# Half of one store and the loads of one block move behind a tile's first visit, a value load and a second store behind its second visit (retention, then a cosine-gated MLP)

## The chip, the cores and the metric

The kernel runs on one core of one Trainium2 chip. The metric is the device time of that core in microseconds. TensorE (PE in the profile) multiplies matrices, VectorE (DVE) and GpSimd (POOL) do element-wise work, ScalarE (ACT) does activations and copies, and SyncE (SP) only issues DMAs here.

## What is computed

The reference, cut to its core (q, k, v are 8 batches x 8 heads x 576 positions x 64, in float32; `w_in` is 512x2048 and `w_out` 2048x512):

```python
scores = q @ k.transpose(0, 1, 3, 2) / sqrt(64)
ret = scores * Dmat                      # Dmat[h, i, j] = gamma_h ** (i - j) for i >= j, else 0
x = (ret @ v).transpose(0, 2, 1, 3).reshape(4608, 512)
h = x @ w_in
out = (h * cos(h)) @ w_out               # 4608 x 512, float32
```

## The kernel before, in words

**Blocks and tiles.** The 4608 tokens are cut into 18 blocks of 256 (`j`) for the retention and into nine tiles of 512 (`n`, 0 to 8 in the code; the text calls them by this index) for the MLP. Tile n computes its MLP from the retention outputs of blocks 2n and 2n+1, and while it does so the retention of two later blocks, 2n+2 and 2n+3, is finished.

**The retention of a block.** `load` (L133) brings q, k and v of a block into SBUF, from a pool `ld` that holds three blocks. `prep` (L217) scales q and k by powers of gamma on GpSimd (four instructions at L203), and `round_v` (L210) casts v to bfloat16 there (two instructions at L214). `turned` (L225) transposes the scaled q and k on TensorE. `scores` (L287), `sums_of` (L351) and `outputs` (L492, made of `out_own` L433 and `out_carried` L471) are short matmuls with 64-row operands; the matmul at L477 is the last kind of an output.

**The MLP of a tile.** `mm1` (L511) makes h, 64 matmuls of 512 columns per tile (L525); cosine (L538) and product (L539) follow on ScalarE and VectorE. The second product is done by `mm2_seven` (L658) with seven products of quarter matrices in place of eight, in the order x = 1, 2, 6, 4, 7, 5, 3, each of 16 matmuls of 256 columns (L640). Their sums give four output tiles: c11, c21, c22 and u1 (tile buffers `ot`, two for each of the four). ScalarE copies a product out (L670), VectorE adds another to it (L666), and `stored_rows` (L650) writes the tile out by two DMAs of 64 partitions each.

**Where the visits lie.** In tiles 3 to 7 the transposes stand ahead of product 2. The retention's short matmuls stand in two packets, which the code calls a unit and this text a visit: the first (`first_unit`, L1051) ahead of product 4, and the second (`second_unit`, L1054) ahead of product 3, or of 5 in tile 7. A visit issues an output's own part, the state sums and scores of another block, and the output's carried part.

**What sets the order.** Each engine runs its instructions in the order in which the program records them; that order is written by hand. Adds and stores that wait for a product are put in a list `pend` and recorded by `flush`. After c11's store (s = 0) `stored` calls `steps_to` (L767), which records `prep`, `round_v` and the next block's load; the store of u1 (s = 3) does this a second time. All loads and nearly all stores are issued from SP's one queue, so a store that waits for its sum holds back whatever is recorded behind it. Around the first visit the order on SP is thus: both halves of c11's store, loads of q, k and v, then both halves of the stores of c21, of c22 and of u1, then the loads of the other block. Loads exist up to tile 5; then all 18 blocks are in.

Of the kernel before, what the change touches and what calls it, by code (L numbers as in the profile page):

```python
# [17 lines left out]
def kernel(  # L18
# [9 lines left out]
    nc = tc.nc  # L28
# [4 lines left out]
    HP = P // 2  # L33
# [9 lines left out]
    N2 = DM // 2  # L43

    W = 512
    NT = NTOK // W
    last = NT - 1
    BK = 256
    NB = NTOK // BK
# [44 lines left out]
    tiles = {}  # L94
# [23 lines left out]
    def parts_of(t0, n, per):  # L118

        cut = -t0 % S  # L120
        if 0 < cut < n:
            return [(0, cut // per, t0), (cut // per, n // per, t0 + cut)]
        return [(0, n // per, t0)]

    def after(i, gate):
        tc.add_manual_dep(
            i.ins,
            gate.ins.name,
            mybir.DependencyInfo(mybir.DependencyClass.Sync, mybir.DependencyReason.DATA),
            reason="in this order",  # L130
        )

    def load(j, names="qkv", gate=None):  # L133
        for name in names:
            src = {"q": q, "k": k, "v": v}[name]
            if name == "q" or j < NP_B:
                f = ld.tile([P, H, 2, D], F32, tag="f" + name, name=f"f{name}")
                for p0, p1, t in parts_of(j * BK, BK, 2):
                    b, s0 = divmod(t, S)
                    i = nc.sync.dma_start(  # L140
                        f[p0:p1].rearrange("p h r d -> p h (r d)"),
                        src[b, :, s0 : s0 + 2 * (p1 - p0), :].rearrange(
                            "h (p r) d -> p h (r d)", r=2
                        ),
                    )
                    if gate is not None:
                        after(i, gate)
                        gate = None
            else:
                f = ld.tile([P, 2, H, D], F32, tag="f" + name, name=f"f{name}")  # L150
                for y in range(2):
                    for p0, p1, t in parts_of(j * BK + y * P, P, 1):
                        b, s0 = divmod(t, S)
                        i = nc.sync.dma_start(
                            f[p0:p1, y],
                            src[b, :, s0 : s0 + p1 - p0, :].rearrange("h s d -> s h d"),
                        )
                        if gate is not None:
                            after(i, gate)
                            gate = None  # L160
            tiles["f" + name, j] = f
        return i
# [109 lines left out]
    def head(he, hg):  # L272
        return he * HG + hg

    def q_cols(c, he, hg, n):
        return tiles["qkT", c.j][he * D : he * D + D, 0, :, hg, c.p0 : c.p0 + n]
# [194 lines left out]
    def out_carried(j, ps):  # L471
        cs = [c for c in chunks[j] if c.carry]
        for hg in range(0, HG, 2):
            for c in cs:
                for h in [head(he, hg + u) for u in range(2) for he in range(2)]:
                    he = h // HG
                    nc.tensor.matmul(  # L477
                        ov_cols(c, ps, h, c.carry),
                        lhsT=s_before[c][he * D : he * D + D, h % HG, :],
                        rhs=q_cols(c, he, h % HG, c.carry),  # L480
                        start=False,
                        stop=hg > 0 and c is cs[-1],
                        skip_group_check=True,
                    )
# [119 lines left out]
    def late_sums(n, xs):  # L604
        for x in xs:
            g_sum(n, x, 6 if x == 5 and n > 1 else 0 if x == 3 and n == 2 else 4, E2)
# [40 lines left out]
            )  # L647
        return parts

    def stored_rows(r0, c0, c1, t, queues=(nc.sync, nc.sync)):  # L650

        rows = out[r0 : r0 + P * t.shape[1], c0:c1].rearrange(
            "(j i r) c -> r i j c", r=2, i=HP
        )
        for r in range(2):
            queues[r].dma_start(rows[r], t[r * HP : (r + 1) * HP])

    def mm2_seven(n, at, stored, xs=(1, 2, 6, 4, 7, 5, 3), early=None):  # L658
        pend = []

        def flush():
            while pend:
                pend.pop(0)()

        def add(out_, in0, in1):
            return lambda: nc.vector.tensor_tensor(out=out_, in0=in0, in1=in1, op=ALU.add)  # L666

        def copied(tag, x):
            t = op.tile([P, 2, N2], F32, tag=tag, name="ot")
            held.append(lambda ps=tiles["all", x]: nc.scalar.copy(t, ps))  # L670
            return t

        def store(t, r, c, s):
            def go():
                queues = (nc.sync, nc.scalar) if n == last and s else (nc.sync, nc.sync)
                stored_rows(n * W + r * 256, c * N2, (c + 1) * N2, t, queues)
                stored(s)

            return go

        def copies():
            while held:
                held.pop(0)()

        for x in xs:
            if x not in at:
                copies()
                flush()
            else:
                if at[x].__name__ in ("nothing", "first_scores", "last_outputs", "turning"):  # L690
                    copies()
                at[x](flush, pend)
                copies()
            if x == 6 and n > 1:
                late_sums(n, (3,))
            parts = product(n, x, early)
            if x == 1:
                c11 = copied("a", 1)
                tiles["c11"] = c11
                if n > 1:  # L700
                    late_sums(n, (5, 6))
            elif x == 2:
                c11 = tiles["c11"]
                if n == 1:
                    p2 = copied("d", 2)
                    continue
                pend[:0] = [add(c11, c11, tiles["all", 2]), store(c11, 0, 0, 0)]
            elif x == 6:
                u1 = copied("b", 1)
            elif x == 4:  # L710
                c21 = copied("c", 4)
            elif x == 7 and n == 1:
                pend += [
                    add(c21, c21, tiles["all", 1]),
                    add(c22, c22, tiles["all", 1]),
                    store(c21, 1, 0, 1),
                    store(c22, 1, 1, 2),
                    add(c11, c11, p2),
                    store(c11, 0, 0, 0),
                ]  # L720
            elif x == 7:
                c22 = copied("d", 1)
                pend += [add(c21, c21, tiles["all", 1]), store(c21, 1, 0, 1)]
            elif x == 5 and n == 1:
                c22 = copied("d", 5)
            elif x == 5 and n == last:
                for (j, c0, c1), ps in zip(parts, tiles["o", 5]):
                    pend.append(add(c22[:, j, c0:c1], ps, c22[:, j, c0:c1]))
                pend.append(store(c22, 1, 1, 2))
            elif x == 5:  # L730
                pend += [
                    add(c22, c22, tiles["all", 5]),
                    add(u1, u1, tiles["all", 5]),
                    store(c22, 1, 1, 2),
                ]
            elif n < last:
                pend += [add(u1, u1, tiles["all", 5 if n == 1 else 3]), store(u1, 0, 1, 3)]
                flush()
            else:
                flush()  # L740
                copies()
                for (j, c0, c1), ps in zip(parts, tiles["o", 5]):
                    add(u1[:, j, c0:c1], ps, u1[:, j, c0:c1])()
                    if c1 == N2:
                        stored_rows(
                            n * W + j * P, N2, DM, u1[:, j : j + 1, :], (nc.sync, nc.scalar)
                        )

    loaded, prepared = 2, 0
# [7 lines left out]
    def step(then_load=True):  # L757

        nonlocal prepared
        if prepared < NB:  # L760
            prep(prepared)
            round_v(prepared)
            prepared += 1
            if then_load:
                load_next()

    def steps_to(j):  # L767
        while prepared < min(NB, j):
            step()

    def load_w_in(e0, part=None):
        dgs = slice(0, DG) if part is None else slice(2 * part, 2 * part + 2)
# [182 lines left out]
    for n in range(NT):  # L955
# [37 lines left out]
        if n == 0:  # L993
# [28 lines left out]
            for done, (t, e) in enumerate(order):  # L1022
# [9 lines left out]
                for u in range(2 * (t == 1) if t < 2 else 1) if e == ET - 1 else ():  # L1032
                    u = u if t < 2 else t
# [78 lines left out]
        else:  # L1112
            at = {2: turning, 4: first_unit, 3 if b + 1 < NB else 5: second_unit} if n < last else {}

        def stored(u):
            if n == 1:
                if u == 0:
                    step(False)
            else:
                steps_to({0: 2 * n + 6, 3: 2 * n + 7}.get(u, 0))  # L1120

        mm2_seven(n, at, stored, *([(2, 4, 6, 5, 7, 3)] if n == 1 else []))

# [29 lines left out]
```

## Time and profile before

| | |
|---|---|
| median of 3 runs | 293.02 us (292.79 to 293.71) |
| the profiled execution's own time | 292.63 us |
| its span, from first to last instruction | 290.9 us |
| TensorE busy | 284.3 us, 98% of the span |
| VectorE, ScalarE, GpSimd busy | 218.5, 170.7, 147.9 us |
| granted TensorE clock | 1.000 |
| DMA traffic | 42.62 MB, mean 146 GB/s |

Shares are of the span. A busy TensorE is not necessarily at its peak, since matmuls overlap; how fast a stage goes is seen from the chain of waits, which lists pieces of work in order of time with their lengths. The profile names a wait by the engine and line that waited and by what ended the wait. Lines with SPq are DMA issues on SP's queue; their length is the time of issuing and not of the transfer.

### The profile page before, as it was taken

The numbers are of one execution on the slowest core, as the hardware profiler recorded it, in microseconds if no ns is written. First come the engines' busy times: TensorE is split into PE (matmuls) and PEld (weight loads), VectorE is DVE, ScalarE is ACT, GpSimd is POOL, SyncE is SP. The second block draws the span as 40 slices with busy tenths as digits, with TensorE's granted clock in tenths as the row PEclk, the third lists the DMA queues.
The fourth block names the chain that finished last, engine by engine and source line by source line (L and its number), as shares of the span: only waits on it lengthen the run. The fifth ranks groups of instructions, "written<-read, shape, count | busy, mean of one in ns | idle before, by whom it ended". The sixth has DMA issues, their size and how long they took to land.

```text
span 290.9 us, 10529 instructions
## 1 busy us (share of the span) xinstructions
PE 284.3 (98%) x4336; PEld 191.3 (66%) x4336; DVE 218.5 (75%) x309; ACT 170.7 (59%) x200; POOL 147.9 (51%) x169
## 2 busy tenths in 40 slices
PE   7999999999999999999999999999999999999994
PEld 2664446888854786478647874687458845884584
DVE  5767758999967967896789677977698669745943
ACT  6756216756677655676467746673767476536620
POOL 7840435698977993379136923593348024002400
PEclk9999999999999999999999999999999999999999
DMA  7999999997997989837690589139101220122013
GB/s 218 275 171 205 252 235 247 224 220 195 223 224 183 268 207 230 210 78 176 170 227 15 129 200 217 42 99 231 38 0 41 65 49 0 41 51 59 0 38 108
DMA packets 103853, 42.62 MB, mean 146 GB/s; under 512 B 68480, under 2 KB 103296, under 8 KB 103808
## 3 DMA queue, kind: packets, MB, share of 16 engines
q1 hardware_dynamic: 99104, 37.37, 52.5%
q0 software_dynamic: 4256, 4.19, 9.1%
q8 instruction: 36, 0.59, 0.8%
q10 hardware_dynamic: 448, 0.39, 0.4%
q14 instruction: 9, 0.07, 0.1%
HBM read 36.70 MB, written 9.44 MB: 159 GB/s over the span
## 4 chain that ended last, share of the span: by engine, by line
PE 94%; DVE 3%; DMA 1%; issue 0%; ACT 0%; DVEq 0%; ACTq 0%
PE h L525 43%; PE o L640 34%; PE o L1025 5%; PE ov L449 3%; PE tr L239 3%; PE ov L477 2%; PE sc L332 2%; DVE ret L312 1%; PE st L365 1%; DMA fk<-in_k_dram 1%; DVE qks L171 1%; PE sc L299 0%; PE tr L260 0%; ACT ot L670 0%; PE idle L270 0%
## 5 line engine op out<-in xcount | busy, mean ns | idle before, releaser
L525 PE MATMUL h<-xT,w_in_sb 128*128 128x512 bf16 (+1 forms) x656 | 127.4, 353 | 0.0
L539 DVE TENSOR_TENSOR gT<-h,cosh 128x1024 bf16<-128x1024 f32 x72 | 87.8, 1221 | 27.3 <-ACT cosh L538 26.8
L538 ACT ACTIVATE cosh<-h,half_pi 128x1024 f32<-128x1024 f32 x72 | 80.2, 1115 | 40.7 <-PE h L525 40.7
L525 PEld LDWEIGHTS <-w_in_sb 128*128 128x128 bf16 x656 | 63.5, 98 | 58.6 <-DMA w_in_sb<-in_moe_w_in_dram 0.2
L579 POOL TENSOR_TENSOR gs<-gT 128x512 bf16<-128x512 bf16 x30 | 38.1, 1271 | 99.6 <-DVE gT L539 99.0
L640 PEld LDWEIGHTS <-gs 128*128 128x128 bf16 x528 | 49.6, 98 | 5.9
L203 POOL TENSOR_TENSOR qks<-fk,gkc 128x512 bf16<-128x512 f32 x32 | 39.0, 1237 | 5.1 <-DMA fk<-in_k_dram 5.1
L640 PEld LDWEIGHTS <-gT 128*128 128x128 bf16 x384 | 36.6, 98 | 6.1
L666 DVE TENSOR_TENSOR ot<-ot,o 128x512 f32<-128x512 f32 x35 | 23.3, 683 | 20.2 <-ACT ot L670 12.6
L245 ACT COPY qkT<-tr 128x1024 bf16<-128x1024 bf16 x29 | 27.7, 1021 | 12.0 <-PE tr L239 11.0
L203 POOL TENSOR_TENSOR qks<-fq,gq 128x512 bf16<-128x512 f32 x28 | 31.2, 1134 | 4.6 <-DMA fq<-in_q_dram 4.6
L640 PE MATMUL o<-w_out_sb,gs 128*128 128x256 bf16 (+1 forms) x264 | 30.7, 270 | 0.0
L640 PE MATMUL o<-w_out_sb,gT 128*128 128x256 bf16 x256 | 30.6, 273 | 0.0
L640 PE MATMUL o<-ws,gs 128*128 128x256 bf16 (+1 forms) x264 | 30.4, 269 | 0.0
L670 ACT COPY ot<-o 128x512 f32<-128x512 f32 x33 | 19.2, 586 | 18.1 <-PE o L640 17.5
L341 DVE TENSOR_TENSOR ret<-sc,mask_c 128x512 bf16<-128x512 f32 x32 | 20.6, 683 | 7.5 <-PE sc L332 6.6
L214 POOL CAST vb<-fv 128x512 bf16<-128x512 f32 x35 | 22.0, 650 | 6.7 <-DMA fv<-in_v_dram 6.7
L425 ACT CAST sb<-s_all 128x768 bf16<-128x768 f32 (+2 forms) x17 | 15.6, 919 | 14.0 <-DVE s_all L416 13.9
L416 DVE TENSOR_TENSOR s_all<-st,s_all 128x256 f32<-128x256 f32 x49 | 20.7, 422 | 1.9 <-PE st L365 0.6
L496 ACT CAST xT<-ov 128x1024 bf16<-128x1024 f32 x16 | 16.2, 1012 | 9.6 <-PE ov L477 9.4
L579 DVE TENSOR_TENSOR gs<-gT 128x512 bf16<-128x512 bf16 (+1 forms) x24 | 15.8, 660 | 0.6
L579 DVE TENSOR_TENSOR gs<-gs,gT 128x1024 bf16<-128x1024 bf16 x16 | 15.2, 948 | 0.3
(83 smaller groups left out, 213.7 us busy)
## 6 DMA issues: line engine op xcount, KB each, us to landing
out_dram<-ot SPq DMA_DIRECT2D x68, 128.0 KB, 2.7
fk<-in_k_dram SPq DMA_DIRECT2D x28, 256.0 KB, 5.3
fv<-in_v_dram SPq DMA_DIRECT2D x28, 256.0 KB, 4.8
fq<-in_q_dram SPq DMA_DIRECT2D x12, 512.0 KB, 5.0
w_out_sb<-in_moe_w_out_dram POOLq DMA_DIRECT2D x4, 512.0 KB, 9.6
fq<-in_q_dram SPq DMA_DIRECT2D x4, 384.0 KB, 7.3
fk<-in_k_dram SPq DMA_DIRECT2D x2, 512.0 KB, 5.0
fv<-in_v_dram SPq DMA_DIRECT2D x2, 512.0 KB, 5.9
```

The costliest lines, as they stand in the source:

```text
L203: return eng.tensor_tensor(out=dst.rearrange("p b a d -> p a b d"), in0=src.rearrange("p (a b) d -> p a b d", a=2), in1=by.rearrange("p (a ...
L214: runs[y](vb[:, y], f[:, :, y, :] if j < NP_B else f[:, y])
L245: lambda r=r: evacs[r](tiles["qkT", j][:, :, :, :, r * HP : r * HP + HP], pss[r])
L341: nc.vector.tensor_tensor(out=ret[:, he].rearrange("p b y i -> p (b y) i"), in0=ps[he].rearrange("p b y i -> p (b y) i"), in1=mask_c.unsqu ...
L416: nc.vector.tensor_tensor(out=s32[:, u], in0=ps[c.half][:, c.y], in1=s32[:, u - 1] if u else tiles["run"], op=ALU.add,)
L525: nc.tensor.matmul(ps[:, j, :], lhsT=w_in_sb[:, dg, (et + j) * P : (et + j + 1) * P], rhs=xT[:, dg, c0 : c0 + w], start=dg == 0 and not (i ...
L538: nc.scalar.activation(cosh, ps, ACTF.Sin, bias=half_pi, scale=1.0)
L539: nc.vector.tensor_mul(gT[:, et : et + m, c0 : c0 + w], ps, cosh)
L579: i = eng.tensor_tensor(out=tiles["gs", n, x][:, e : e + step], in0=a[:, e : e + step], in1=b[:, e : e + step], op=op_,)
L640: nc.tensor.matmul(dst[i], lhsT=lhs[:, e, j * P : (j + 1) * P], rhs=rhs[:, e, c0:c1], start=(fresh and e == 0 and (i == 0 or len(parts) > 2)),
L666: return lambda: nc.vector.tensor_tensor(out=out_, in0=in0, in1=in1, op=ALU.add)
L670: held.append(lambda ps=tiles["all", x]: nc.scalar.copy(t, ps))
```

## The change

In tiles 3 to 7, the second half of c11's store is recorded behind the first visit and waits for that visit's last carried matmul; its first half stays. In tiles 3 to 5, which still load, the loads of q and k of the block follow it there. The load of v and, in tiles 3 to 6, the store of c21 are recorded behind the second visit, and so behind c22's store. The block's loads are thus taken out of the step that records its `prep`. The core of the diff:

```diff
-                    nc.tensor.matmul(
+                    tiles["end"] = nc.tensor.matmul(
                         ov_cols(c, ps, h, c.carry),
...
-    def stored_rows(r0, c0, c1, t, queues=(nc.sync, nc.sync)):
+    def stored_rows(r0, c0, c1, t, queues=(nc.sync, nc.sync), halves=(0, 1), gate=None):
...
-        for r in range(2):
-            queues[r].dma_start(rows[r], t[r * HP : (r + 1) * HP])
+        for r in halves:
+            i = queues[r].dma_start(rows[r], t[r * HP : (r + 1) * HP])
+            if gate is not None:
+                after(i, gate)
+                gate = None
...
+        late = {4: [], 3: []}
+
         def store(t, r, c, s):
+            where = n * W + r * 256, c * N2, (c + 1) * N2, t
+
             def go():
-                queues = (nc.sync, nc.scalar) if n == last and s else (nc.sync, nc.sync)
-                stored_rows(n * W + r * 256, c * N2, (c + 1) * N2, t, queues)
-                stored(s)
+                if 2 < n < last and s == 0:
+                    stored_rows(*where, halves=(0,))
+                    late[4].append(lambda: stored_rows(*where, halves=(1,), gate=tiles["end"]))
+                    stored(s, late)
+                elif 2 < n < last - 1 and s == 1:
+                    late[3].append(lambda: stored_rows(*where))
+                else:
+                    queues = (nc.sync, nc.scalar) if n == last and s else (nc.sync, nc.sync)
+                    stored_rows(*where, queues)
+                    stored(s)
...
                 at[x](flush, pend)
                 copies()
+                for run in late.pop(x, ()):
+                    run()
...
-    def steps_to(j):
+    def steps_to(j, late=None):
+        nonlocal loaded
         while prepared < min(NB, j):
-            step()
+            step(late is None)
+            if late and loaded < NB:
+                late[4].append(lambda j=loaded: load(j, "qk"))
+                late[3].append(lambda j=loaded: load(j, "v"))
+                loaded += 1
```

More of the change, by code (lines that the diff above doesn't have):

```diff
@@ L1113, with stored @@
             at = {2: turning, 4: first_unit, 3 if b + 1 < NB else 5: second_unit} if n < last else {}
-        def stored(u):
+        def stored(u, late=None):
             if n == 1:
@@ L1119, in stored @@
             else:
-                steps_to({0: 2 * n + 6, 3: 2 * n + 7}.get(u, 0))
+                steps_to({0: 2 * n + 6, 3: 2 * n + 7}.get(u, 0), late)
         mm2_seven(n, at, stored, *([(2, 4, 6, 5, 7, 3)] if n == 1 else []))
```

## The prediction

> **What bounds the kernel now.** I read the page first: its busy times, then the shares of the chain that ended last.
>
> ```profile
> PE 284.3 (98%) x4336; PEld 191.3 (66%) x4336; DVE 218.5 (75%) x309; ACT 170.7 (59%) x200; POOL 147.9 (51%) x169
> ...
> PE 94%; DVE 3%; DMA 1%; issue 0%; ACT 0%; DVEq 0%; ACTq 0%
> ```
>
> TensorE is busy 98% of the span and is 94% of the chain. The rest, waits for the first loads and for VectorE, lies by the chain in order of time ahead of 17.45 us, at 70.1 us (ScalarE, 0.59) and at the very end, outside tiles 3 to 7. The next view is the busy time by stretches, one for each tile that the change touches (tiles 3 to 7, bounds from the chain).
>
> ```profile
> core 0: us, PE busy (x) PEld busy (x) DVE busy (x) ACT busy (x) POOL busy (x), PEclk, DMA share, GB/s
> 111.87:141.93 30.06, 30.06 (x489) 20.48 (x488) 23.47 (x32) 19.11 (x22) 16.44 (x16) 1.00 0.72 174
> 141.93:171.91 29.98, 29.98 (x482) 20.40 (x480) 23.46 (x32) 19.00 (x22) 16.44 (x16) 1.00 0.57 139
> 171.91:201.92 30.01, 30.01 (x482) 20.39 (x480) 23.39 (x32) 19.00 (x22) 16.44 (x16) 1.00 0.60 146
> 201.92:231.88 29.96, 29.96 (x481) 20.38 (x480) 23.34 (x32) 19.00 (x22) 11.32 (x10) 1.00 0.16 39
> ```
>
> The first number behind the bounds is the length, the next PE's busy time: they are equal in each row, at a granted clock of 1.00. The reader should compare the fourth row with the others: tile 6 loads nothing (DMA share 0.16 against 0.57 to 0.72) and is only 0.02 to 0.10 us shorter. The chain in order of time shows tile 3's visits and the products between them (start, length, what).
>
> ```profile
> 128.47 3.60 PE o L640 x32
> 132.07 0.25 PE ov L449 x16
> 132.32 0.26 PE st L365 x32
> 132.57 0.29 PE sc L332 x32
> 132.87 0.27 PE ov L449 x15
> 133.13 0.29 PE ov L477 x31
> 133.43 5.34 PE o L640 x48
> ```
>
> The first visit lasts 133.43 - 132.07 = 1.36 us, with PE work throughout. The 48 products behind it take 5.34 us here, with the DMA share at 0.98 by the stretches view (133.43 to 138.77), and 5.35 us in tile 6, at 0.08 (223.41 to 228.76). The place to look next is therefore the queue that the change rearranges. The first three lines are SP's queue, the other three GpSimd's, one tile later, where the block that is loaded here is used.
>
> ```profile
> 131.22 1.26 SPq L656 DMA_DIRECT2D out_dram<-ot  x2
> 132.57 1.37 SPq L140 DMA_DIRECT2D fq<-in_q_dram  x2
> 136.00 2.47 SPq L154 DMA_DIRECT2D fv<-in_v_dram  x2
> ...
> 157.89 2.22 POOL L203 TENSOR_TENSOR qks<-fq,gq 128x512 bf16<-128x512 f32 x2
> 160.07 2.94 POOL L203 TENSOR_TENSOR qks<-fk,gkc 128x512 bf16<-128x512 f32 x2
> 162.96 1.17 POOL L214 CAST vb<-fv 128x512 bf16<-128x512 f32 x2
> ```
>
> GpSimd had no wait for a DMA anywhere between 111.9 and 261 us: its only one in the waits view is for VectorE's gT (70.9 us in all).
>
> **The change part by part**, in tile 3; tiles 4 and 5 are alike, about 30 us later each.
>
> *Store of c11, second half.* Its issue at 131.87 (half of the first line) moves to the visit's end, 133.43, plus the increment to SP: 1.6 us later. Nothing reads the output, and its buffer is written again two tiles, 60 us, later. PE's and every other computing engine's instructions stay in the order they had; only SP gets a wait more. Cost 0.
>
> *Loads of q and k.* They follow that half, which takes 0.63 us to issue (1.26 / 2), so q starts at 133.43 + 0.63 = about 134.1 in place of 132.57, 1.5 us later. Queued behind SP's new wait are just these and the stores after them. q landed 5.5 us after its first issue began at the latest (138.10 against 132.57), so it will be there near 140, for a use at 157.89: some 18 us of cover. For k, at 135.4 to 137.5 and with the 4.6 us that the DMA view gives its issues to landing, it is 142 against 160.07.
>
> *Load of v and store of c21.* They now wait for c22's store, whose sum ends at about 139.5 (two VectorE adds from 138.81, 1.28 us in all). Two issues of c22 take 1.26, so v begins at about 140.8 in place of 136.00, 4.8 us later. Its two issues take 2.47 and its landing at most 5.6 us (the longest of the v loads in the trace from 111 to 201 us): 148.9 against 162.96, 14 us of cover. The store of c21 goes from 138.56 to 143.3. Nobody waits for it.
>
> *What comes behind on SP.* Before, u1's store waited until 143.63 for its sum, so part of the delay disappears in that wait: 143.3 + 1.3 for c21 gives 144.6, 1.0 us later. The other block's loads slip from 144.97 to about 146, its last landing from 153.96 to 155, and its v is cast at 168.1: 13 us. The next tile's first store is issued at 161.28, after an idle queue. So the delay doesn't add up from tile to tile. In tiles 6 and 7 there is nothing to load, and a late store remains: 0.
>
> *A gain from moved traffic.* The bound is tile 6 with hardly any traffic: (30.06 - 29.96) + (29.98 - 29.96) + (30.01 - 29.96) = 0.17 us if all of it went away. It's moved, not removed; I take 0. A loss has the same bound in the products, where a DMA share of 0.98 cost nothing (5.34 against 5.35).
>
> *Instruction blocks.* One thing that DMAs bring to PE doesn't stand in its waits: its instructions.
>
> ```profile
> q8 instruction: 36, 0.59, 0.8%
> ```
>
> That is 36 packets of 16 KB (0.59 MB / 36). The DMA view has one between 133.7 and 135 and the next between 140.3 and 142. In the trace's packet records they start at 133.87 and 140.43 and take 0.99 and 1.49 us; over all 36 it is 0.88 to 1.55. The first of the two already runs among the loads of q and k, the second among those of v. After the change both do so again, about as densely. No stretch shows PE waiting, so I take 0 and keep the other end as a rival below. [...]
>
> **The sum** is 0 (-0.17 to 0 where rows bound it) on the profiled execution's 292.63 us. That execution lies 0.39 us below the median of the runs, 293.02, which I carry over: forecast **293.0 us**.
>
> **The rivals.**
>
> [...]
>
> *Faster: the visit starts more smoothly.* In the waits view for weight loads between 111.9 and 261 us there is one small thing at the visits:
>
> ```profile
> PEld L449 <- issue: 2.3, 11, 0.2
> ```
>
> That is 11 times 0.21 us, for no reason that the profile sees. Were SP's traffic the cause, and the wait a delay of PE, the five first visits would give back 5 x 0.21 = 1.05 us: 292.0. Against it: the second visits and tile 7, which loads nothing, have it too, and PE's own row has no gap then.
>
> *It does not do what it says.* The loads could be held up by something else, so that the order on SP changes and their times don't. The built program has the second half wait on PE in five tiles, and k behind it in three; the time would be 293.0 all the same.
>
> **How the numbers follow.** About 0.3%, 0.9 us, is what a measurement of this kernel can tell from no change (the three runs lie 0.92 us apart). Forecast, with the last rival in it: 0.74. The late block, from 0.9 us up: 0.15, because one unseen resource is left. The smoother visit, 0.9 us or more: 0.11; the packed chain speaks against it more than against a loss that no row could show. The range goes from the faster rival, 292.0, to the slower one's near end, 294.4; its far end stays out.
>
> **What would show it.** Right: in the changed profile the tiles last 30.0 us within 0.1, SP's second half is issued near 133.5, q near 134.1, v near 140.8, GpSimd waits for no load from 111.9 to 261 us, and the visits keep 1.3 us. Wrong: a gap in PE or a longer piece at L640 just after a first visit, with q8 packets far over 1.5 us (late block); first visits shorter than 1.26 us, with the 0.21 us gone (faster); or a POOL wait for fv or fq, which would mean that 14 us of cover were misread.

## The result, and the profile after

The changed kernel takes 292.07 us (median of 22 runs, 291.36 to 293.81); the kernel before, run beside it, 292.96 us (22 runs, 292.26 to 293.88). The ratio is 0.9972, with a 95% interval of 0.996 to 0.9984: faster by 0.28%, just under the 0.3% that the prediction had named as its bound for "the same". The forecast of 293.0 us and its range held, the range by 0.07 us only. The forecast was a gain of nothing, though, and the profile shows that this was wrong. One execution among the experiments, of the kernel with the second visit's part alone, took 1126 us at a granted clock of 1.00; no other number rests on it.

The spans hide it: 290.7 us against 290.9. In the changed kernel's profile, tile 3 begins 0.96 us later (112.83 against 111.87), because a load of q at the start ended late (7.53 us of the chain, ahead of anything that was changed). The busy time by stretches, tile 3 to tile 7, tells what the change did:

```profile
core 0: us, PE busy (x) PEld busy (x) DVE busy (x) ACT busy (x) POOL busy (x), PEclk, DMA share, GB/s
112.83:142.61 29.78, 29.78 (x489) 20.27 (x488) 23.30 (x32) 19.12 (x22) 16.42 (x16) 1.00 0.65 154
...
202.08:231.82 29.74, 29.74 (x482) 20.22 (x480) 23.38 (x32) 18.98 (x22) 11.31 (x10) 1.00 0.22 55
```

Tile 3 went from 30.06 to 29.78 us, tile 6, which loads nothing, from 29.96 to 29.74. The five tiles together went from 149.16 to 148.02: 1.14 us less. The chain in order of time says where, here for tile 3's two visits and the products between them:

```profile
133.03 0.25 PE ov L449 x16
133.27 0.26 PE st L365 x32
133.53 0.29 PE sc L332 x32
133.82 0.13 PE ov L449 x15
133.96 0.29 PE ov L477 x31
134.25 5.35 PE o L640 x48
139.60 0.25 PE ov L449 x16
139.84 0.26 PE st L365 x32
140.10 0.29 PE sc L332 x32
140.40 0.13 PE ov L449 x15
140.53 0.23 PE ov L477 x23
140.75 0.33 PE o L640 x2
```

Compare the fourth line with that of the prediction: the second group at L449 took 0.27 us before and takes 0.13 now. The products are as they were (5.35 against 5.34). Read by the start of each matmul, every visit before had one place at which its next matmul started 0.08 to 0.14 us after the last, where 0.04 or less is usual: nine visits, nine such gaps, and no wait beside any of them. (The step from a visit's last matmul to the product behind it, 0.12 us before and after, is not counted.) After the change there is none in these nine. Summed from the first start of a visit to the first start of the product behind it:

| visits | before | after |
|---|---|---|
| five first ones, tiles 3 to 7 | 6.52 us | 5.96 us |
| four second ones, tiles 3 to 6 | 5.20 us | 4.64 us |

That is 0.56 + 0.55 = 1.11 of the 1.14 us.

SP's queue shows what left the visits. Before, the second half of c11's store was issued from 131.87 to 132.47, with the visit from 132.00 on. After:

```profile
132.17 2.76 SPq L656 DMA_DIRECT2D out_dram<-ot  x2
135.03 1.69 SPq L140 DMA_DIRECT2D fq<-in_q_dram  x2
136.81 1.20 SPq L154 DMA_DIRECT2D fk<-in_k_dram  x2
140.35 2.10 SPq L656 DMA_DIRECT2D out_dram<-ot  x2
142.54 1.29 SPq L154 DMA_DIRECT2D fv<-in_v_dram  x2
```

The first line holds both halves, with the wait between them: the first half ends at 132.78, 0.17 us ahead of the visit, and the second starts at 134.34, behind it. No issue ends inside this visit, nor inside the second.

### The profile page after: what moved, and what is told of

Its sections match the earlier page's. It is cut to its first block, busy times and chain, and to the rows that moved or that the text cites. A ratio compares the mean times of both kernels' runs of the same rounds, so it can differ in the third digit from the quotient of the medians.

```text
span 290.7 us, 10530 instructions
## 1 busy us (share of the span) xinstructions
PE 283.5 (97%) x4336; PEld 190.5 (66%) x4336; DVE 218.9 (75%) x309; ACT 170.6 (59%) x200; POOL 147.1 (51%) x169
## 4 chain that ended last, share of the span: by engine, by line
PE 86%; DVE 7%; DMA 4%; issue 1%; ACT 0%; DVEq 0%; ACTq 0%
PE h L525 40%; PE o L640 34%; PE o L1046 3%; PE tr L239 3%; DMA fq<-in_q_dram 3%; PE ov L449 3%; DVE gT L539 2%; DVE ret L312 1%; PE ov L477 1%; PE sc L332 1%; DMA fk<-in_k_dram 1%; PE st L365 1%; DVE qks L171 1%; DVE w_out_sb L557 1%; DVE ws L557 1%; DVE s_all L416 1%
## 5 line engine op out<-in xcount | busy, mean ns | idle before, releaser
L214 POOL CAST vb<-fv 128x512 bf16<-128x512 f32 x35 | 21.4, 637 | 6.7 <-DMA fv<-in_v_dram 6.5
L640 PE MATMUL o<-ws,gT 128*128 128x256 bf16 x128 | 15.3, 273 | 0.0
```

The source lines that it names most:

```text
L214: runs[y](vb[:, y], f[:, :, y, :] if j < NP_B else f[:, y])
L640: nc.tensor.matmul(dst[i], lhsT=lhs[:, e, j * P : (j + 1) * P], rhs=rhs[:, e, c0:c1], start=(fresh and e == 0 and (i == 0 or len(parts) > 2)),
```

## The experiments

**Theories.** I: an issue that SP works on during a visit stops TensorE's supply of instructions, and shows as a gap once TensorE has used up what it had in hand. T: the bytes that move slow TensorE down. C: the boundaries of TensorE's instruction blocks make the gaps. The blocks are the 36 packets of 16 KB on q8; that they are TensorE's is inferred, for 8672 of the 10529 profiled instructions are its matmuls and weight loads. A place in a visit is given as the time since its first matmul's start.

**The first visit's part alone.** `late[3].append(... load(j, "v"))` becomes `late[4]`, and c21's store is not moved:

```diff
-                elif 2 < n < last - 1 and s == 1:
+                elif False:
```

> Only the part at the first visit: c11's second half and the loads of q, k and v behind it; c21's store stays where it was. Visits are measured from their first matmul's start to the first start of the product behind them; before, the five first visits of tiles 3 to 7 take 1.27 to 1.36 us and the four second ones of tiles 3 to 6 1.27 to 1.32; in the changed kernel 1.18 to 1.23 and 1.16. Theory I (a DMA issue on SP that ends 0.3 to 0.7 us after a visit's start stops PE's supply of instructions once, for some 0.1 us, about 0.26 us after its end): first visits 1.18 to 1.23, second visits still 1.27 or more, since v and c21 are issued in them; tiles 3 to 7 about 0.55 us shorter than before, ratio about 0.998. Theory T (moved bytes slow PE): the first visits gain too, the second visits lose more than before, as v now moves in them as well. Theory C (instruction blocks alone): no visit changes, ratio 1.000.

Measured: ratio 0.9987 (0.9966 to 1.0008), 292.3 us; in the profile tiles 3 to 7 take 148.14 us, 1.02 less. The first visits sum to 5.95 us: clean. Of the second ones, those of tiles 3 to 5 were clean too, which I had not expected, and that of tile 6 kept its gap (1.26 us). Two stretches of this kernel, the second visits of tiles 3 and 6:

```profile
139.05:140.25 1.20, 1.20 (x122) 1.14 (x122) 1.07 (x2) 0.19 (x1) 0.63 (x2) 1.00 1.23 267
228.25:229.55 1.30, 1.30 (x122) 1.24 (x122) 1.17 (x2) 0.19 (x1) 0.00 (x0) 1.00 0.26 60
```

The visit with 267 GB/s is the clean one, that with 60 GB/s the one with a gap. T falls. In the first, an issue of v, of 128 partitions, ended 0.43 us into the visit, but had taken 1.79 us; in the second a store's issue of 64 partitions and the usual 0.60 us ended at 0.29.

**The second visit's part alone.** c11 is stored and q and k are loaded as before; v and c21 move. The second label is the same kernel once more, with a profile of its own.

> Only the part at the second visit: v's load and c21's store behind it; both halves of c11's store and q and k as before. Theory I: second visits of tiles 3 to 6 at 1.16 us, each first visit still 1.27 to 1.36 with one gap of about 0.1 us; tiles 3 to 6 together about 0.6 us shorter, ratio about 0.998; the sum of this and of the other part is the whole change's 1.1 us. Theory T: the second visits of tiles 3 and 4, during which q and k may still move, gain less than that of tile 6, which has no loads. Theory C: no visit changes.

> The part at the second visit alone, looked at once more for its profile. Theory I, as the first runs leave it (an issue on SP of its usual 0.6 to 0.8 us that ends 0.3 to 0.8 us into a visit costs PE about 0.1 us, and the gap closes 0.385 us after the issue's end; an issue stretched to 1 us and more by a full queue mostly costs nothing): first visits of tiles 3 to 7 at 1.27 to 1.36 us with a gap that closes near 0.86, second visits of tiles 3 to 6 at 1.16. Theory T: the second visits lie between, as q and k still move in those of tiles 3 and 4.

Measured: ratio 0.9984 (0.9969 to 0.9998), 292.46 us. In the second label's profile tiles 3 to 7 take 148.55 us, 0.61 less; all second visits are at 1.16 us, and all first ones have their gap (1.27 to 1.36). The parts add to 1.63 us, more than the whole's 1.14, because the first part alone cleans three second visits as well, by the way in which it shifts v's issues.

**A small piece in the visit.** c11's first half in two pieces, `ps=(0, 60)` as before and `ps=(60, HP)` with `gate=tiles["m", 6, 12]` (the 13th of product 6's 16 matmuls).

> The changed kernel, but the first half of c11's store is cut into 60 partitions, issued as before, and 4 partitions (8 KB) that wait for product 6's 13th matmul, so that this one issue ends about 0.45 us into each first visit of tiles 3 to 7, where c11's second half ended before the change. Theory I: the size doesn't matter, each of the five first visits has a gap of about 0.1 us near 0.75 us and takes 1.27 us or more again; second visits stay at 1.16. Theory T: 8 KB move next to nothing, so the first visits stay at 1.18 to 1.23.

Measured: the first visits stay at 1.18 to 1.23 us. It settles nothing on size: the issue of 4 partitions took some 0.28 us, not 0.6, and ended at 0.03 to 0.07 us, too early to tell. The run "dose" below comes back to it.

**Another place for the same issue.** `gate=tiles["m", 6, 2 * n + 2] if n < 7 else tiles["begin"]`.

> The changed kernel with c11's second half (64 KB by partitions, as in the change) waiting for another matmul in each tile: tiles 3, 4, 5 and 6 for the 9th, 11th, 13th and 15th of product 6, tile 7 for the first of the visit. The issue should end at about 0.00, 0.22, 0.43, 0.65 and 0.9 us after the visit's start. In tiles 3 to 5 the load of q is issued right behind it and ends a second issue some 0.65 us later or more. Theory I: a gap follows the end of an issue by 0.26 us: near 0.7 us in tile 5, near 0.9 in tile 6, none in tile 7 (1.16 is past the end); in tiles 3 and 4 the first issue falls into the time in which PE still has instructions ahead, and q's issue, ending near 0.65 and 0.87, makes the gap near 0.9 to 1.1. Theory T: the gap, if any, follows the first packets, and tile 7 has one too. Theory C: the gap stays at one place or is in no tile.

Measured (the half is 128 KB by the DMA view, not 64): the waits of tiles 3 to 5 were over before SP's queue was free, so that all three issues ended at 0.52; tile 6's ended at 0.59, tile 7's at 0.84. Gaps of 0.080, 0.087, 0.098 and 0.112 us ended at 0.90, 0.91, 0.91 and 0.97, in tile 7 there was none: the visit was over. q's issues, which end behind 1.1, made none, but a gap of theirs would also have come too late to show. So the gap goes with the issue: it closes 0.38 to 0.39 us after the issue's end, and in the nine visits before 0.38 to 0.40 us after it.

**Boundaries of blocks shifted.** The kernel before with 128 filler instructions more in tile 2. If every block holds the same number of instructions, which is assumed, the blocks from tile 3 on begin 128 instructions elsewhere, about half of what a visit has (120 or 128 matmuls, each with its weight load).

```diff
-    fillers = {0: 96, 1: 80, 2: 80, 3: 126,
+    fillers = {0: 96, 1: 80, 2: 208, 3: 126,
```

> [...] Theory I: the issues' ends fall as before, so first and second visits of tiles 3 to 7 keep their gaps, 1.26 us or more each. Theory C (the boundary alone makes the gap, or the boundary and an issue together): the boundary leaves the visits or moves in them by half their instructions, and gaps vanish or move by more than 0.3 us; visits without one take 1.16 to 1.23.

Measured: 295.08 us in one run; tile 3 starts 3.5 us later, since tile 2 got slower, but tiles 3 to 7 take 148.14 us, 1.02 less than before. Eight visits of nine are clean, which seemed to speak for C. SP's queue says otherwise. The whole store, both halves, and then its second half alone:

```profile
134.68 1.99 SPq L656 DMA_DIRECT2D out_dram<-ot  x2
```
```profile
135.34 1.33 SPq L656 DMA_DIRECT2D out_dram<-ot  x1
```

The second half took 1.33 us to issue in place of 0.60, and a fetch of an instruction block now starts beside it (in the five tiles, 0.2 us before to 0.03 us after the issue's start). It so ends 1.2 us into the visit, too late for a gap in it. The one visit whose issue kept its 0.60 us, tile 6's second, kept its gap with the blocks shifted, and at the same place; in the chain it is the 0.42 us of the scores (0.40 before the shift), which take 0.29 in a clean visit:

```profile
231.81 0.42 PE sc L332 x32
```

C alone is refuted. Until here I had expected that any issue in a visit stops TensorE. Now theory I needs a second half. I took it to be length: an issue of the usual 0.60 us does, and a stretched one of 0.9 us or more doesn't, with one exception. That was not shown: the stretched halves here end too late to tell, and the stretched issues that ended in time were loads of 128 partitions. The run "Dose, between 48 and 64" below says what fits better.

**The half on ScalarE's queue.** The late second half is issued on ScalarE's queue in place of SP's, without the wait; q and k get `gate=tiles["end"]` themselves.

```diff
-                    late[4].append(lambda: stored_rows(*where, halves=(1,), gate=tiles["end"]))
+                    stored_rows(*where, (nc.sync, nc.scalar), halves=(1,))
```

> The changed kernel with the second half of c11's store issued from ScalarE's queue instead of SP's, without a wait for the visit; q and k wait for the visit's end themselves, so that SP issues nothing inside it. ScalarE comes to that issue about 0.2 us before the visit, which ends it about 0.4 us into it. Theory I, any queue: a gap near 0.7 us in the first visits of tiles 3 to 7, 1.27 us or more. Theory I, SP's queue alone: no gap, 1.18 to 1.23, unless ScalarE's flag copy comes later and makes PE wait for it. Theory T: a gap, as the same bytes move.

Measured: 292.42 us in one run; the issue took 0.64 to 0.75 us but ended 0.03 to 0.23 us ahead of the visit, not in it. So it tells nothing of ScalarE's queue. It tells of bytes: both halves now travel during the visit, with a DMA share of 0.58 where the kernel before had 0.53.

```profile
132.73:133.90 1.17, 1.17 (x129) 1.13 (x130) 0.31 (x1) 0.68 (x2) 1.17 (x2) 1.00 0.58 145
```

All five first visits are clean (1.18 to 1.23 us): T is refuted a second time, here at 145 GB/s in a clean visit, above at 267.

**The whole store late.** Is it any use to keep the first half early?

```diff
-                    stored_rows(*where, halves=(0,))
-                    late[4].append(lambda: stored_rows(*where, halves=(1,), gate=tiles["end"]))
+                    late[4].append(lambda: stored_rows(*where, gate=tiles["end"]))
```

> The changed kernel with both halves of c11's store behind the first visit. Theory I: the first half's issue ended 0.17 us ahead of the visit and did no harm, or little; first visits within 0.05 us of the changed kernel's, time within 0.1% of it, ratio to before about 0.997. Theory T: a half fewer in the visits, first visits shorter by another 0.02 to 0.06 us, to 1.16.

Measured: ratio 0.9974 (0.9961 to 0.9988), 292.39 us: the same as the change within their intervals, with first visits at 1.18 to 1.23 us in both. The half that stays early does no harm, since its issue ends ahead of the visit (by 0.17 us in tile 3 of the changed kernel). The later queue puts an issue of k (64 partitions, 0.655 us, ending at 0.34) into tile 4's second visit, which then has a gap of 0.117 us and lasts 1.29.

**Dose.** `size` partitions of the second half are issued in the visit, another number in each tile, and the rest behind it, as are q and k.

```diff
-                    late[4].append(lambda: stored_rows(*where, halves=(1,), gate=tiles["end"]))
+                    size = {3: 4, 4: 16, 5: 32, 6: 48, 7: 64}[n]
...
+                        gate = tiles["begin"] if n == 3 else tiles["m", 6, 15 if n == 4 else 14]
+                        stored_rows(*where, halves=(1,), gate=gate, ps=(0, size))
+                        if size < HP:
+                            stored_rows(*where, halves=(1,), gate=tiles["end"], ps=(size, HP))
```

> The changed kernel with a part of c11's second half issued in the first visit and the rest of it behind: 4, 16, 32, 48 and 64 partitions in tiles 3, 4, 5, 6 and 7, each waiting for a matmul so that its issue ends 0.4 to 0.6 us into the visit (4 partitions took 0.28 us to issue, 64 take 0.60; linear between them 0.34, 0.43 and 0.52). Theory I with PE's supply slowed for as long as SP works on an issue: no gap for 4 and 16 partitions, a small one or none for 32, 0.05 to 0.1 us for 48, about 0.1 for 64, visits from 1.18 to 1.30 us. Theory I with a fixed stop at the end of each issue: five gaps of about 0.1 us, whatever the size, each visit 1.27 us or more. Theory T: the gap follows the bytes in flight, none for 4 partitions, growing with size, and at the place of the packets, 0.4 us and more behind the issue's start, not locked to its end.

Measured: issues of 0.34, 0.36, 0.47, 0.46 and 0.60 us that end at 0.58, 0.46, 0.46, 0.45 and 0.59. The first four make no gap (visits of 1.25, 1.18, 1.18, 1.18 us), the last makes one of 0.116 us (1.31). Here are 48 partitions in tile 6, SP's issue and the chain of the same visit, and then 64 in tile 7:

```profile
222.23 0.46 SPq L658 DMA_DIRECT2D out_dram<-ot  x1
```
```profile
223.19 0.29 PE ov L479 x30
```
```profile
251.50 0.59 SPq L658 DMA_DIRECT2D out_dram<-ot  x1
```
```profile
252.46 0.42 PE ov L479 x31
```

The issues end at 0.45 and 0.59, and the last part takes 0.29 us in the one and 0.42 in the other; the 4 partitions of tile 3 also end at 0.58 and make no gap. That refutes a fixed stop at the end of every issue. Theory I in its simple form would have the gap grow with the issue, as 0.60 us less some 0.49 us that TensorE has in hand (an estimate from this issue and its gap of 0.116). That fits 0.60 us, but not what the other visits of these runs have: issues of 0.77 to 0.81 us made gaps of 0.12 to 0.14, not of 0.3.

**A load in the visit.** q's first issue is released by `tiles["m", 6, 13]`; the store's second half and k come behind the visit.

```diff
-                late[4].append(lambda j=loaded: load(j, "qk"))
-                late[3].append(lambda j=loaded: load(j, "v"))
+                late[4].append(lambda j=loaded: load(j, "q", gate=tiles["m", 6, 13]))
+                late[3].append(lambda j=loaded: load(j, "kv"))
```

> The changed kernel with the load of q issued inside the first visits of tiles 3 to 5 in place of c11's second half (q waits for product 6's 14th matmul, its first issue ends about 0.4 to 0.5 us into the visit; the half store waits for the visit's end, k goes behind the second visit with v). Theory I for any issue on SP: a gap of 0.05 to 0.1 us that closes 0.385 us after q's issue, first visits of tiles 3 to 5 at 1.25 us or more, of tiles 6 and 7 at 1.18. Theory I for stores alone: tiles 3 to 5 stay at 1.18 to 1.23. Theory T: slower than with the store, for q moves four times the bytes.

Measured, in one run: 292.88 us. In tile 3 q's issue took 0.63 us and the visit has a gap of 0.115 us (1.36); in tiles 4 and 5 it took 0.53 and 0.54 and there is none (1.18). So it is not a matter of stores. Length seems to decide again, but the three issues, of one line of code, are not alike. The DMA view has their sizes, first tile 3, then tiles 4 and 5:

```profile
fq<-in_q_dram SPq DMA_DIRECT2D x1, 256.0 KB
fq<-in_q_dram SPq DMA_DIRECT2D x1, 384.0 KB, 4.8
fq<-in_q_dram SPq DMA_DIRECT2D x1, 512.0 KB
```

A block that crosses from one batch to the next is loaded in pieces. At 4 KB of q in a partition, these are 64, 96 and 128 partitions: the smallest of the three made the gap.

**Dose, between 48 and 64.** As above with `size = {3: 52, 4: 56, 5: 60, 6: 62, 7: 63}[n]` and `tiles["m", 6, 14]` in all.

> As the run before with parts of c11's second half, now with 52, 56, 60, 62 and 63 partitions in the first visits of tiles 3 to 7, all waiting for product 6's 15th matmul (issue from about 0.01 us ahead of the visit's start). There 48 partitions took 0.46 us to issue and made no gap, 64 took 0.60 and made one of 0.116 us. If PE's supply stands still for as long as SP works on the issue, the gap is the issue's length less what PE has in hand, about 0.49 us: 0 to 0.01 for an issue of 0.50, 0.04 for 0.53, 0.07 for 0.56, 0.1 for 0.59. If it is a stop of fixed length that only long issues make, the gap jumps from 0 to 0.1 at one size.

Measured: 0.50, 0.46, 0.48, 0.32 and 0.29 us, for the length doesn't follow the number of partitions; no gap in any (1.18 to 1.23 us). None of these issues took more than 0.50 us, so whether the gap grows from nothing or begins at a threshold stays open.

The profiles taken together say more: the number of partitions separates all cases, where length leaves two over. In the visits of 120 and 128 matmuls, in tiles 2 to 7 of all these profiles but the one of 1126 us, 35 issues of 64 partitions on SP ended 0.29 to 0.81 us into a visit, stores and loads of q, k and v alike; a gap followed each of them. Of 23 issues of 4 to 63, 96 or 128 partitions that ended there, none made a gap. The two cases that length leaves over fit: an issue of k took 0.62 us and made no gap (128 partitions), and one of v took 0.90 us and made one of 0.07 us (64 partitions). This is a reading of the runs and not a test made for it: no run changes the number at one length, none has a short issue of 64 partitions, and why it should be 64 is not known.

**The same issue on ScalarE's queue, once more.** With a wait that was to make it fall into the visit; q and k wait for the visit's end, as before.

```diff
-                    late[4].append(lambda: stored_rows(*where, halves=(1,), gate=tiles["end"]))
+                    gate = tiles["m", 6, {3: 11, 4: 12, 5: 11, 6: 12, 7: 12}[n]]
+                    stored_rows(*where, (nc.sync, nc.scalar), halves=(1,), gate=gate)
```

> The changed kernel, but the second half of c11's store is issued on ScalarE's queue, released by the twelfth or the thirteenth of the sixteen matmuls ahead of the first visit, so that an issue of 0.64 us ends about 0.3 to 0.45 us into the visit. If an issue on any queue stops TensorE's supply, each first visit of tiles 3 to 7 has a gap of about 0.11 to 0.15 us that closes 0.38 us behind the issue's end, and lasts 1.27 to 1.36 us; nothing moves on SP, whose issues stay outside the visits. If it is a matter of SP's issues alone, the first visits stay at 1.18 to 1.23 us. A wait of the second group at L449 for ScalarE's copy, which is queued behind the issue, would be another cause, and would show as a wait for ACT in the chain.

Measured: 291.81 us in one run, tiles 3 to 7 in 148.04; the issue again ended ahead of the visit, by 0.03 to 0.23 us. The wait did nothing: c11's store is recorded ahead of product 6, so that `tiles["m", 6, ...]` still names the matmul of the tile before, long done, and the issue starts where it did without a wait, 0.78 us ahead of the visit in tile 3. All visits of these tiles are clean, but the question isn't answered: whether an issue on another queue does the same stays open.

## Why the prediction was right and wrong

**The moves cost nothing: right.** The second half is issued 0.09 us behind the visit's last matmul (134.34 after 134.25), q 0.69 us after that. GpSimd waits for no load from 112 to 261 us, so the 18 and 14 us of cover held. Only v came about 0.9 us later than worked out, as the issue of c22's second half beside a block fetch took 1.42 us.

**The sum of 0: wrong, by 1.11 us in the visits.** By the prediction's own signs the tiles were to last 30.0 us within 0.1 and the visits to keep 1.3 us; tiles 3 to 6 last 29.73 to 29.78, the visits 1.16 to 1.23. The step that failed is "A gain from moved traffic", where the bound was tile 6 "with hardly any traffic", 0.17 us for all tiles. Tile 6 loads nothing, but it stores c11 and c21 as the others do, and their issues lay in its visits. It was no clean row: it gained 0.22 us itself. Rows that are alike showed only that they had the same cost, and a share of bytes was the wrong measure for a cost of issues. The trace of before did have a clean row: tile 2's first visit, also of 120 matmuls, took 1.16 us (from 103.89) without a gap, against 1.27 to 1.32 in the visits of 120 that the change cleared. An issue ended in it as well, one of v, but of 128 partitions (0.92 us).

**"With PE work throughout": wrong.** A matmul of these lasts 0.19 us by itself, so TensorE's busy time covers a gap of 0.08 to 0.14 us, and so do busy times by stretch and the waits. It shows in the starts of the matmuls, and in the chain as a group that is longer than its equals: in the prediction's own lines 15 matmuls at L449 take 0.27 us where 16 of them take 0.25 at the visit's other end, and 0.13 in a clean one.

**The smoother visit (0.11): its time was right, its reason not.** It gave 292.0 us for 292.07, from the 0.21 us waits of the weight loads. These are still there, 11 of them:

```profile
PEld L449 <- issue: 2.3, 11, 0.2
```

SP's traffic was the cause, as that rival assumed, but by the issues, and of both visits: 0.56 and 0.55 us instead of 1.05 in the first ones. That the time came out was luck.

**The late block (0.15): did not happen.** No visit and no product behind one has a stall: the 48 products behind the first visits of tiles 3 to 6 take 5.34 to 5.35 us, before and after. The 1.4 us between the forecast and the range's upper end of 294.4 were the price of a TensorE that stops for a fetch that comes late, and no run shows such a stop. The fetches in tiles 3 to 7 of the changed kernel took 0.93 to 1.43 us. What took longer beside a fetch was an issue on SP: stores' issues that began during one took 1.30 to 1.42 us in the changed kernel, and 0.82 to 1.93 over all profiles, where 0.60 is usual.

**The range held**, by luck, as its lower end was the time of that rival, and with 0.28% the change lies just inside the 0.3% that were called the same. The interval, 0.16% to 0.4%, doesn't decide on which side of that bound it lies.

**Open:** why an issue on SP holds up TensorE, why those of 64 partitions and not the others, whether length plays a part beside, and whether an issue on another queue does it. That it is the supply of instructions is inferred: nothing on TensorE waits there, and the gap follows the issue in time. No kernel was clearly better than the change.

## What to carry to other kernels

In a dense stretch of short matmuls, read the distances between their starts and not the busy time, and compare a stretch with one that is free of DMA issues, not of bytes. Here it was worth keeping issues of 64 partitions on SP out of them (a gap in 35 cases of 35); a wait on the stretch's last matmul did that, and cost nothing where the loads had 14 and 18 us to spare. A row is a bound for a cost only if it lacks the suspected cause.

## What was not expected of the hardware

- An issue of 64 partitions on SP's queue that ended 0.29 to 0.81 us into a visit of 120 matmuls or more left a gap in 35 cases of 35; issues of 4 to 63, 96 or 128 partitions did in none of 23. The gap is 0.06 to 0.14 us (once 0.36) and closes 0.38 to 0.41 us after the issue's end in 33 of the 35.
- How long an issue took did not follow the number of its partitions in proportion: stores of 4, 16, 48, 52, 62, 63 and 64 partitions took 0.26 to 0.34, 0.36, 0.46, 0.50, 0.32, 0.29 and 0.60 us.
- A store's issue of 64 partitions that began while a packet of 16 KB of instructions (q8) was under way took 0.82 to 1.93 us, in 58 cases of 58 (from 100 us on); most of those beside which the fetch began later kept some 0.60 us.
